# Scaling the fourth x tile of the opening on GpSimd in place of DVE

## The chip, the cores and the metric

The kernel runs on one core of one Trainium2 chip. The metric is the device time of one execution in microseconds (us); the median of several runs is given. The engines are named as the profile names them: PE (TensorE), ACT (ScalarE), DVE (VectorE), POOL (GpSimd) and SP, which here only issues DMAs.

## The reference

The kernel computes an attention block with a cached set of keys and values, gated by a SwiGLU block, with a residual:

```
xn = layernorm(x)                                  # x: 2048 x 640, bf16
q  = xn @ wq                                       # 32 heads of 192
p  = softmax(q @ k^T * 192**-0.5)                  # 2048 cached keys for each head
s  = concat_heads(p @ v) @ wo
g  = silu((silu(xn @ w1) * (xn @ w3)) @ w2)        # hidden width 1536
out = x + s * g
```

The layer norm is (x - mean) / sqrt(var + eps) for each row, without weights.

## The kernel before, in words

The 2048 rows of x are 16 tiles of 128 rows (`x_all[:, i, :]`). Each tile is normalised, turned so that its 640 columns stand on the partitions, and kept as `xnT[:, i]`; all projections read `xnT`. A query block (`qb`) is four tiles, 512 rows. The first four tiles are needed before any product can start, so the opening does them by themselves, and in another way than the other twelve:

- **Statistics.** Tiles 0, 2 and 3 get their mean and variance on DVE (`ln_stats`, `bn_stats` at L237 and `bn_aggr` at L240), tile 1 on ACT (L279 to L281). They land in `mv`.
- **Root.** `ln_root` (L246, L249) makes 1 / sqrt(var + eps) on ACT, for two tiles at a time: `ln_root(0)` for tiles 0 and 1, `ln_root(2)` for tiles 2 and 3.
- **Scaling.** `ln_scale(i)` (L257) computes (x - mean) * root in one `tensor_scalar` with two operations, a tile of 128x640 bf16 into a tile `xn` of the same shape. This is the step of the change.
- **Turning.** `ln_turn` makes five PE transposes for each tile (L264) into PSUM (`pst`); then ACT copies tiles 0 and 2 and DVE tiles 1 and 3 into `xnT` (L265).

Until the first tile is scaled, PE runs products of constants (`keep_busy`, L226). After the 20 transposes it goes on to the first products of head 0 (`pq`, `pf`, L318), first with tiles 0 and 1, then with tiles 2 and 3. The other tiles are scaled on DVE by the same function and turned by a DMA (`scale_and_turn`, L268).

The attention works on one head and one query block at a time, in eight steps (`p`) of 256 keys: scores on PE (`st`, L505) into one of two PSUM buffers, exponential on ACT (`pT`, L512), values on PE (`obank`, L545). The exponential subtracts a bound `nb` for the scores' maximum. For the first block of head 0, the bound comes from a small PE product (L438). For head 1, whose first block follows right behind, it comes from `next_bound(1, 0)`: two small DVE operations (L445, L448) and a sum over the partitions on GpSimd (`partition_all_reduce`, L451). This sum is one of GpSimd's loadable instructions; the kernel loads the library that has it at L73, as GpSimd's first instruction:

```
sums = next(x for x in all_libraries if bass_isa.InstPartitionAllReduce in x.instructions)
pin(nc.gpsimd.load_library(sums))
```

GpSimd has other work in the opening: it clears `st` (L163), puts ones into the values (L151), copies half of the keys to the other 64 partitions (`KS`, L154, in two halves for each of the first two heads) and rows of the queries (L379, L385).

`pin` keeps instructions in the order in which the code is written, for each engine. So the order of the opening is written out by hand, and an instruction of GpSimd's queue waits for all ahead of it. A load of a library for an instruction that needs another one than the last is put in by the language, right ahead of that instruction.

Of the kernel before, what the change touches and what calls it, by code (L numbers as in the profile page):

```python
# [30 lines left out]
def _kernel_impl(ctx, tc, A_x, A_k_cache, A_v_cache, A_wq, A_wo, B_w1, B_w3, B_w2, out):  # L31
    nc = tc.nc
# [33 lines left out]
    pin = tc.keep_in_program_order  # L66
# [108 lines left out]
    with ExitStack() as actx:  # L175
# [12 lines left out]
        mv = lnx.tile([P, NQT, nc.vector.BN_AGGR_DIM], F32, name="mv")  # L188
        x_all = lnx.tile([P, NQT, D], BF16, name="x_all")
# [52 lines left out]
        rstd = {}  # L242
# [9 lines left out]

        scaled = {}

        def ln_scale(i):
            scaled[i] = xnp.tile([P, D], BF16, tag="xn", name="xn")
            pin(nc.vector.tensor_scalar(out=scaled[i][:], in0=x_all[:, i, :], scalar1=mv[:, i, 0:1], scalar2=rstd[i],  # L257
                                        op0=ALU.subtract, op1=ALU.mult))

        def ln_turn(i, pool, tag, cp):  # L260
# [9 lines left out]
        def scale_and_turn(i):  # L270
            ln_scale(i)
            dma_turn(i)
# [16 lines left out]
        keep_busy(1, behind=ln_stats(3, lambda seen: keep_busy(1, behind=seen)))  # L289
        ln_root(2)  # L290
        for i in range(4):
            ln_scale(i)
        turned = []
        for i in range(4):
            pool, tag = (ps_st, "st2") if i < 2 else (ps_o, f"ob{3 - i}")
# [849 lines left out]
@with_exitstack  # L1145
def kernel(
    ctx: ExitStack,
    tc: tile.TileContext,
    A_x: bass.AP,
    A_k_cache: bass.AP,  # L1150
    A_v_cache: bass.AP,
    A_wq: bass.AP,
    A_wo: bass.AP,
    B_x: bass.AP,
    B_w1: bass.AP,
    B_w3: bass.AP,
    B_w2: bass.AP,
    out: bass.AP,
):
    _kernel_impl(ctx, tc, A_x, A_k_cache, A_v_cache, A_wq, A_wo, B_w1, B_w3, B_w2, out)  # L1160
# [30 lines left out]
```

## Time and profile before

| | us |
|---|---|
| median of 3 runs | 1932.29 (1932.17 to 1932.43) |
| profiled execution, own time | 1932.65 |
| its span, first to last instruction | 1931.1 |
| PE busy | 1924.4 |
| ACT busy | 1275.8 |
| DVE busy | 950.1 |
| GpSimd busy | 447.5 |

The granted TensorE clock was 1.0 over the span. Times in the views are counted from the start of the span. A row in order of time gives start, length, engine, line, operation, output and inputs, a count where like instructions are merged, and in brackets the idle time ahead of it and what ended it. A row of a group gives a count, busy time, mean ns of one, idle time and what ended it. A row of a source line gives the shortest, median and longest duration in ns and the first and last start. Rows marked with a q (POOLq) belong to the engine's sequencer and not to its busy time.

### The profile page before, as it was taken

What the parts mean: (1) busy time and instruction counts of PE and PEld (TensorE: products, weight loads), DVE (VectorE), ACT (ScalarE), POOL (GpSimd) and SP (SyncE); (2) the same over time, 40 slices, a digit from 0 to 9 for tenths busy, and PEclk for the clock granted to TensorE, in tenths of its full rate; (3) what the DMA queues carried; (4) which work ended last, traced back from release to release, by engine and by line L of the source; (5) the groups of instructions that cost most, each with busy time, mean ns of one, the idle gap of its engine ahead of it and who ended that gap; (6) DMA issues with size and microseconds to landing.
All of it is one profiled execution on the core that took longest, in us unless ns stands there. A gap on an engine that the chain in (4) does not pass through costs nothing.

```text
span 1931.1 us, 59187 instructions
## 1 busy us (share of the span) xinstructions
PE 1924.4 (100%) x26595; PEld 1266.7 (66%) x26621; DVE 950.1 (49%) x1794; ACT 1275.8 (66%) x1284; POOL 447.5 (23%) x756
## 2 busy tenths in 40 slices
PE   9999999999999999999999999999999999999999
PEld 6666666666666666666666666666777777444444
DVE  7765545554545554545555555555554544421111
ACT  7777777777777777777777777777777777210000
POOL 2432222222222222223222222222222210000000
PEclk9999999999999999999999999999999999999999
DMA  8422223131212222222422222213121102868752
GB/s 170 94 71 50 72 41 79 41 80 42 63 38 59 49 63 52 58 77 71 104 53 68 50 71 50 71 42 80 42 80 37 37 10 75 268 105 165 158 114 61
DMA packets 336835, 145.36 MB, mean 75 GB/s; under 512 B 286688, under 2 KB 330400, under 8 KB 336576
## 3 DMA queue, kind: packets, MB, share of 16 engines
q1 hardware_dynamic: 320592, 113.37, 25.8%
q0 software_dynamic: 7744, 23.60, 4.3%
q10 hardware_dynamic: 8240, 4.56, 0.8%
q8 instruction: 209, 3.42, 0.7%
q14 instruction: 50, 0.41, 0.1%
HBM read 56.23 MB, written 31.98 MB: 46 GB/s over the span
## 4 chain that ended last, share of the span: by engine, by line
PE 99%; DMA 0%; DVE 0%; issue 0%; SPq 0%
PE obank L545 35%; PE st L505 34%; PE ps L345 14%; PE ps_s L925 8%; PE ps_f L973 2%; PE ps_t L934 2%; PE ps_gu L318 1%; PE ps_s L948 1%; PE ps_gu L345 1%; PE ps_f L983 0%; DMA x_all<-in_A_x_dram 0%; DVE st L237 0%; PE pst L264 0%; PE pq L318 0%; PE pb L325 0%
## 5 line engine op out<-in xcount | busy, mean ns | idle before, releaser
L512 ACT ACTIVATE pT<-st,nb 128x1024 bf16<-128x1024 f32 x960 | 1068.5, 1113 | 327.6 <-PE st L505 323.8
L545 PEld LDWEIGHTS <-pT 64*128 64x128 bf16 x16384 | 717.5, 94 | 238.6 <-ACT pT L512 0.4
L545 PE MATMUL obank<-vt,pT 64*128 64x193 bf16 x16384 | 854.3, 243 | 0.0
L521 DVE TENSOR_REDUCE osum<-obank 128x386 f32<-128x772 f32 x256 | 234.2, 956 | 640.3 <-PE obank L545 640.3
L505 PE MATMUL st<-qF,KT 64*128 64x512 bf16 x1024 | 385.0, 376 | 0.0
L505 PE MATMUL st<-qD,KT 64*128 64x512 bf16 x1024 | 385.0, 376 | 0.0
L505 PE MATMUL st<-qS,KT 64*128 64x512 bf16 x1024 | 384.9, 376 | 0.0
L505 PE MATMUL st<-qS,KS 64*128 64x512 bf16 x1024 | 384.9, 376 | 0.0
L505 PE MATMUL st<-qA,KS 64*128 64x512 bf16 x1024 | 384.8, 376 | 0.0
L505 PE MATMUL st<-qA,KT 64*128 64x512 bf16 x1024 | 384.8, 376 | 0.0
L505 PEld LDWEIGHTS <-KT 64*128 64x128 bf16 x4096 | 288.5, 94 | 134.2
L345 PE MATMUL ps<-xnT,w 64*128 64x512 bf16 (+1 forms) x2540 | 313.5, 374 | 0.0
L379 POOL COPY qS<-qA 64x512 bf16<-64x512 bf16 x255 | 158.5, 622 | 564.6 <-ACT qA L389 555.1
L345 PEld LDWEIGHTS <-w 64*128 64x128 bf16 x2540 | 123.9, 94 | 116.9
L505 PEld LDWEIGHTS <-KS 64*128 64x128 bf16 x2048 | 177.0, 94 | 7.6
L925 PE MATMUL ps_s<-wo_sb,oT 128*128 128x512 bf16 x704 | 156.8, 379 | 0.8
L528 DVE TENSOR_TENSOR ostage<-osum,rl_all 128x384 bf16<-128x384 f32 x256 | 142.8, 558 | 8.9
L925 PEld LDWEIGHTS <-oT 128*128 128x128 bf16 x720 | 70.4, 98 | 84.5
L154 POOL COPY KS<-KT 64x1024 bf16<-64x1024 bf16 (+1 forms) x68 | 68.6, 1009 | 232.7 <-DMA KT<-in_A_k_cache_dram 200.6
L108 POOL DMA_DIRECT2D w<-in_A_wq_dram x60 | 52.9, 882 | 289.8 <-PE ps L345 289.6
L390 DVE CAST qF<-ps 128x512 bf16<-128x512 f32 x120 | 83.0, 691 | 72.3 <-ACT qA L389 72.3
L890 DVE SCALAR_TENSOR_TENSOR tmp<-ps_s,g_all 128x512 f32<-128x512 f32 x16 | 11.0, 688 | 177.4 <-PE ps_s L925 168.2
(112 smaller groups left out, 1148.6 us busy)
## 6 DMA issues: line engine op xcount, KB each, us to landing
o_scr<-ostage SPq DMA_DIRECT2D x64, 384.0 KB, 2.7
vt<-in_A_v_cache_dram SPq DMA_DIRECT2D x60, 384.0 KB, 5.0
wo_sb<-in_A_wo_dram POOLq DMA_DIRECT2D x1, 7680.0 KB, 31.1
w<-in_A_wq_dram POOLq DMA_DIRECT2D x30, 160.0 KB, 3.6
hT_scr<-hblk SPq DMA_DIRECT2D x16, 256.0 KB, 3.0
xt<-in_A_x_dram POOLq DMA_DIRECT2D x8, 320.0 KB, 4.4
w<-in_B_w_dram POOLq DMA_DIRECT2D x30, 80.0 KB, 2.6
w<-in_A_wq_dram POOLq DMA_DIRECT2D x30, 80.0 KB, 3.0
```

The lines of the kernel that those rows point to most:

```text
L108: return lambda eng: keep(eng.dma_start(out=w[:, :, c0:c1], in_=src[:, s0:s0 + c1 - c0].rearrange("(c p) d -> p c d", p=P)))
L154: return [keep(nc.gpsimd.tensor_copy(out=KS[ROWS[r], c0:c1], in_=ks[ROWS[1 - r], 2 * r, c0:c1])) for r in range(2)]
L345: mm = pin(nc.tensor.matmul(out[:, t * 512 + t0 * P:t * 512 + (t0 + step) * P], lhsT=ws[t][ROWS[r], c, :], rhs=rows_of(qb, c, ROWS[r], t0, ...
L379: return [lambda t=t: keep(copy(out=hd["qS"][ROWS[t], qs], in_=hd["qA"][ROWS[1 - t], qs])) for t in range(2)]
L390: pin(cast(out=hd["qF"][:, qs], in_=ps[:, 512:1024]))
L505: pin(nc.tensor.matmul(st2[:, t * 512:(t + 1) * 512], lhsT=k[ROWS[t]], rhs=q[ROWS[t], qs], start=(s == 0), stop=(s == 2)))
L512: pin(nc.scalar.activation(out=pT2[:, c0:c1], in_=st2[:, c0:c1], func=ACT.Exp, scale=SCALE, bias=nb))
L521: pin(nc.vector.tensor_reduce(out=osum[:], in_=ob[:].rearrange("p t (j c) -> p j c t", j=2)[:, :, 0:DH + 1, :], axis=AX.X, op=ALU.add))
L528: pin(nc.vector.tensor_tensor(out=ostage[:, b * 2:b * 2 + 2, hg * DH:(hg + 1) * DH], in0=osum[:, :, 0:DH], in1=rl.unsqueeze(2).to_broadcas ...
L545: pin(nc.tensor.matmul(acc["o"][b][:, r, j * 256:j * 256 + DH + 1], lhsT=pT2[ROWS[r], t * 512 + i * P:t * 512 + (i + 1) * P], rhs=vt[ROWS[ ...
L925: pin(nc.tensor.matmul(wide[t], lhsT=oT[:, j, t * P:(t + 1) * P], rhs=wo_sb[:, k, 0:WIDE], start=(k == 0), stop=(k == OC - 1)))
L934: pin(nc.tensor.matmul(turned, lhsT=wo_sb[:, k, WIDE:D], rhs=oT[:, j, 0:w], start=(k == 0), stop=(k == OC - 1)))
```

## The change

`ln_scale` gets a parameter for the engine, and the opening passes GpSimd for tile 3. Nothing else in the code changes.

```
-        def ln_scale(i):
+        def ln_scale(i, eng=nc.vector):
             scaled[i] = xnp.tile([P, D], BF16, tag="xn", name="xn")
-            pin(nc.vector.tensor_scalar(out=scaled[i][:], in0=x_all[:, i, :], scalar1=mv[:, i, 0:1], scalar2=rstd[i],
+            pin(eng.tensor_scalar(out=scaled[i][:], in0=x_all[:, i, :], scalar1=mv[:, i, 0:1], scalar2=rstd[i],
                                         op0=ALU.subtract, op1=ALU.mult))
...
         for i in range(4):
-            ln_scale(i)
+            ln_scale(i, nc.gpsimd if i == 3 else nc.vector)
```

On DVE, in the opening, `rstd_205` is the root of tiles 2 and 3 and `pst` the PSUM tile of the transposes (- is before, + is the change):

```order
 L240 BN_AGGR mv<-st_197 128x2
 L257 TENSOR_SCALAR xn<-x_all,mv,rstd_195 128x640 x2
-L257 TENSOR_SCALAR xn<-x_all,mv,rstd_205 128x640 x2
+L257 TENSOR_SCALAR xn<-x_all,mv,rstd_205 128x640
 L265 COPY xnT<-pst 128x640 x2
 L412 TENSOR_REDUCE st<-KT 128x1
```

One scaling is gone, and DVE comes to its two copies one instruction sooner.

On GpSimd, from its first instruction after the start of the kernel; `L73 ISA` is the load of the library with the partition sum, and `KS<-KT` is the copy of head 0's keys:

```order
 L73 ISA
 L163 MEMSET st 128x16 x2
+L257 ISA
+L257 TENSOR_SCALAR xn<-x_all,mv,rstd_205 128x640
 L151 MEMSET vt 128x16
 L154 COPY KS<-KT 64x512 x2
```

The scaling stands ahead of the memset and of the copies. With it comes an `ISA` row, which is an instruction of the same kind as the one at L73 and loads library 0, while L73 loads library 1.

On GpSimd, around its first partition sum (`nb_all<-ns` is the sum for the first block of head 1, the copies are those of the two halves of head 1's keys):

```order
 L151 MEMSET vt 128x16
 L154 COPY KS<-KT 64x512 x2
+L451 ISA
 L451 ISA nb_all<-ns 128x1
 L154 COPY KS<-KT 64x512 x2
```

The added `ISA` row loads library 1 again, ahead of the first sum and behind the copies of the first half of head 1's keys. The queues of PE, ACT and SP, SP's DMAs among them, are the same in both programs.

## The prediction

> **What bounds the kernel now.** I read the page first, then the chain of work that ended last, cut to the first 30 us, then the order of time around the fourth tile and around GpSimd's first partition sum. The page:
>
> ```profile
> span 1931.1 us, 59187 instructions
> PE 1924.4 (100%) x26595; PEld 1266.7 (66%) x26621; DVE 950.1 (49%) x1794; ACT 1275.8 (66%) x1284; POOL 447.5 (23%) x756
> PE 99%; DMA 0%; DVE 0%; issue 0%; SPq 0%
> ```
>
> TensorE (PE) is busy all the time and is 99% of the chain. So the sum is simple: whatever makes PE wait comes back almost whole in the time, and whatever frees DVE or GpSimd (POOL) at 49% and 23% is worth nothing unless PE was waiting for it. The profiled execution took 1932.65 us, 1.6 us of it outside the span; the median of the runs is 1932.29 us, 0.36 lower. I sum against 1932.65 and take 0.36 off at the end.
>
> The chain in the opening, in order of time (start, length, what):
>
> ```profile
> 7.28 0.39 PE fill L226
> 7.67 1.46 PE pst L264 x20
> 9.14 0.03 issue
> 9.17 0.71 PE pq L318 x5
> ```
>
> PE turns the four x tiles (L264, 20 transposes) and goes on to the first products without a gap. All 20 transposes stand ahead of the products, so the fourth tile's scaling has no cover: each 0.1 us by which it is late makes all that follows 0.1 us late. Around it:
>
> ```profile
> 7.14 1.49 DVE L257 TENSOR_SCALAR xn<-x_all,mv,rstd 128x640 bf16<-128x640 bf16 x4
> 7.59 0.20 ACT L249 ACTIVATE rstd<-lv 128x2 f32<-128x2 f32 x1
> 7.59 1.54 PE L264 MATMUL pst<-ident_bf,xn 128*128 128x128 bf16 x20
> 8.54 0.48 DVE L265 COPY xnT<-pst 128x640 bf16<-128x640 bf16 x1
> ```
>
> DVE scales the four tiles back to back and ends at 7.14 + 1.49 = 8.63. The root that the third and fourth need is there at 7.59 + 0.20 = 7.79.
>
> **The change part by part.** DVE loses one scaling, 1.49 / 4 = 0.37 us. That saves nothing by itself: DVE's copy at 8.54 could start sooner, but the products that read it stand behind the fourth tile's transposes.
>
> GpSimd gets the scaling. Its nearest rows are its copies:
>
> ```profile
> L154 POOL COPY KS<-KT 64x1024 bf16<-64x1024 bf16 x60 | 63.8, 1063 | 220.5 <-DMA KT<-in_A_k_cache_dram 196.9 <-PE ps L345 22.2
> L154 POOL COPY KS<-KT 64x512 bf16<-64x512 bf16 x8 | 4.9, 608 | 12.2 <-DVE xnT L265 8.3 <-DMA KT<-in_A_k_cache_dram 3.6
> ```
>
> 512 columns more cost 0.455 us, so a copy of 640 columns would be 0.608 + 128 x 0.89 ns = 0.72 us. That is the lower end; twice that per column, for two operations, gives 0.15 + 2 x 0.57 = 1.3 us as the upper end. I take 0.9, nearer to the rows that exist. With the root at 7.79 and nothing else in the way the tile would be ready between 8.55 and 9.15, so -0.1 to +0.5 us against 8.63, +0.1 with my value.
>
> The part that decides is something the diff doesn't show. The built program has two more rows on GpSimd that load a library: one ahead of the scaling, one ahead of the first partition sum (L451), which goes back to the library that L73 had loaded. What is known of a load:
>
> ```profile
> L73 POOLq MODIFY_POOL_CONFIG  x2: 11/11/11, 1.1 to 1.1; - x2
> 1.16 0.15 POOL L163 MEMSET st<- 128x16 f32 x2 [0.46 <-POOLq L1175]
> 1.24 0.16 POOL L151 MEMSET vt<- 128x16 bf16 x1
> ...
> 22.18 0.55 POOL L451 PARTITION_ALL_REDUCE nb_all<-ns  x1 [1.52 <-DVE ns L448]
> ...
> 36.53 0.39 POOL L451 PARTITION_ALL_REDUCE nb_all<-ns  x1 [0.37 <-DVE ns L448]
> ```
>
> The load at L73 is two rows of 11 ns at 1.1, and the memsets behind it run at once. Its first user, 21 us on, is 0.55 - 0.39 = 0.16 us longer than the next one. So a load that is real costs anything between about 0.2 us and the 21 us that lie between L73 and 22.18, or L73 loads nothing because the library is still there from the execution before. The second is likelier: no queue but the kernel's own moves anything in the first 16 us.
>
> ```profile
> DMA packets 8999, 3.54 MB, mean 221 GB/s; under 512 B 7975, under 2 KB 8999, under 8 KB 8999
> q1 hardware_dynamic: 8999, 3.54, 97.3%
> ```
>
> In the changed kernel the library really changes twice per execution. [...]
>
> ```profile
> KT<-in_A_k_cache_dram SPq DMA_TRANSPOSE x1, 6.3
> L108 POOL DMA_DIRECT2D w<-in_A_wq_dram x60 | 52.9, 882 | 289.8 <-PE ps L345 289.6 <-issue 0.2
> ```
>
> 6.3 + 0.9 = 7.2 us, an estimate, with 0.2 and 21 kept as the ends. [...]
>
> First load. It stands behind two memsets that end at 1.31 and waits for nothing, so it runs from 1.3 to 8.5, mostly under the statistics. The scaling then runs from 8.5 to 9.4 and the fourth tile is ready 0.8 us later than the 8.63 of before. PE goes on 0.8 us later.
>
> Second load. GpSimd's queue ahead of it, and what waits behind it:
>
> ```profile
> 17.62 0.17 POOL L151 MEMSET vt<- 128x16 bf16 x1
> 19.38 1.27 POOL L154 COPY KS<-KT 64x512 bf16<-64x512 bf16 x2 [1.59 <-DMA KT<-in_A_k_cache_dram]
> ...
> 22.79 1.26 POOL L154 COPY KS<-KT 64x512 bf16<-64x512 bf16 x2
> 24.15 1.11 ACT L512 ACTIVATE pT<-st,nb_all 128x1024 bf16<-128x1024 f32 x1 [0.27 <-PE st L505]
> 25.71 0.38 PE L505 MATMUL st<-qA,KT 64*128 64x512 bf16 x1
> ```
>
> The copies of head 1's keys wait for a transfer until 19.38, with 1.59 us of idle time that absorbs the 0.8, so they still end at 20.65. The load then runs from 20.65 to 27.85, the partition sum from 27.95 to 28.5, and only then can ScalarE (ACT) take the first exponential of head 1, which stood at 24.15. It ends at 28.55 + 1.11 = 29.66. PE, meanwhile, has its old values and the second scores to do, but the third scores need the score buffer that this exponential frees: they start at 29.7 in place of 25.71. That is **+4.0 us**, and it contains the first 0.8, since GpSimd's clock of events is set by the key transfer and not by PE. Generally the sum is the load's length less 3.2 us. The copies behind the sum (22.79, now 28.6 to 29.9) are wanted by the fifth scores of the block, at 28.74 before and 32.7 now: hidden, with 2.8 us to spare. PE has no idle time later in which to win the wait back. Later partition sums find their library in place.
>
> Sum: 1932.65 + 4.0 = 1936.65, or **1936.3** as a median.
>
> **The rivals.** *A switch is nearly free, so not slower.* If a load takes under 3.2 us the partition sum is still ready for 24.15 + 0.8, and if it takes under 6.5 the scaling doesn't wait for it. Then only GpSimd's own pace is left, -0.1 to +0.5, with up to 0.44 more if it must wait for DVE's third tile. A row bears on that:
>
> ```profile
> 11.62 0.29 DVE L379 COPY qS<-qA 64x512 bf16<-64x512 bf16 x1 [1.36 <-ACT qA L596]
> 11.65 0.73 POOL L379 COPY qS<-qA 64x512 bf16<-64x512 bf16 x1 [0.65 <-ACT qA L596]
> 15.74 0.61 POOL L379 COPY qS<-qA 64x512 bf16<-64x512 bf16 x1
> ```
>
> GpSimd's copy beside one of DVE took 0.12 us longer than the same copy alone. [...] Time: 1932.2 to 1933.2, 1932.5 likeliest. For it: 11 ns rows, and no transfer. Against: those rows can be loads that had nothing to do. A gain needs a scaling under 0.8 us; DVE's freed 0.37 us is the most it could be, far under 0.2%, which is about what a measurement of this kernel can tell from no change.
>
> *The load comes only when the first user is called.* Then nothing is hidden: the scaling is called at 7.85, loads until 15.05 and ends at 15.95, 7.3 us late. The partition sum is called when its input is there, 22.0 + 7.3 = 29.3; it loads until 36.5 and ends at 37.05; the exponential ends at 38.2, the third scores start then and not at 25.71 + 7.3 = 33.0, 5.2 more. Together +12.5: 1944.8. For it: the memsets behind L73 weren't held up. Against: the first sum's 0.55 us has no load in it. [...]
>
> *The load at L73 is real too, and the two stand in a row.* Then the second ends at 1.1 + 14.4 = 15.5, the scaling at 16.4, 7.8 us late. GpSimd's queue is behind PE's clock now: copies 25.6 to 26.9, third load until 34.1, exponential until 35.9 against 33.5: 2.4 more. Together +10.2: 1942.5. [...] For it: L73's load could run behind the memsets unseen. Against: no transfer in the queues.
>
> **How the numbers follow.** Forecast 0.42; a free switch 0.20; load at the call 0.18; two in a row 0.15; loads of over 10 us, 0.05. The range goes from the free switch without a gain, 1932.4, to 1944.5, which leaves out the top of the late load, the long loads and the gains, under 2 in 10. 0.2% is 3.9 us, so the line runs through the forecast, at a load of 7.1 us. Slower by over 0.2%: somewhat over half of the forecast (0.24) and all of the last three cases, 0.62. Within: the rest of the forecast and the free switch less the little that I keep for a gain, 0.36. Faster by over 0.2%: 0.02, for nothing that I can name.
>
> **What would show it.** In the changed profile I look for the start of GpSimd's scaling (8.5 by the forecast, 7.8 to 8.3 with a free switch, 15 by the others), the start of the first product (9.17 before, 10.0 by the forecast), GpSimd's first partition sum (22.18 before, 27.95), and ScalarE's idle time ahead of the exponential of 24.15 (0.27 before, some 3.6). The forecast is wrong if the scaling starts after 10 us, or if the exponential waits on PE as before, or if PE's wait at the third scores is given back later, against the 99%.

## The result and the profile after

The changed kernel took 1937.21 us (median of 11 executions, 1935.97 to 1944.30) against 1932.63 us before (11 executions): 1.0028 of the time before, 95% interval 1.0020 to 1.0036. It is slower, by 4.6 us between the medians; the ratio goes by all executions, whose means are 5.4 us apart. The forecast was 1936.3. The profiled execution took 1938.15 us with a span of 1936.5, 5.4 us more than the span before, and the readings below are of that one.

The page's first lines, after:

```profile
span 1936.5 us, 59218 instructions
PE 1928.0 (100%) x26621; PEld 1268.3 (65%) x26621; DVE 949.9 (49%) x1793; ACT 1276.7 (66%) x1284; POOL 451.4 (23%) x757
```

The totals hardly move. The instructions that differ take microseconds, and the time that is lost is idle time, so it has to be looked for in the first 35 us. GpSimd's rows there, after (start, length, engine, line, operation; in brackets the idle time ahead of the row):

```profile
1.16 0.15 POOL L163 MEMSET st<- 128x16 f32 x2 [0.46 <-POOLq L1175]
9.32 2.52 POOL L257 TENSOR_SCALAR xn<-x_all,mv,rstd 128x640 bf16<-128x640 bf16 x1 [8.00 <-ACT xnT L265]
11.80 0.16 POOL L151 MEMSET vt<- 128x16 bf16 x1
...
21.41 1.28 POOL L154 COPY KS<-KT 64x512 bf16<-64x512 bf16 x2
29.63 0.40 POOL L451 PARTITION_ALL_REDUCE nb_all<-ns  x1 [6.94 <-DMA xnT<-xn]
30.09 1.25 POOL L154 COPY KS<-KT 64x512 bf16<-64x512 bf16 x2
```

The two library loads have rows in the engine's sequencer, of 3 to 7 ns, which tell where a load begins and nothing of its length:

```profile
L257 POOLq MODIFY_POOL_CONFIG  x2: 3/5/7, 1.3 to 1.3; - x2
L451 POOLq MODIFY_POOL_CONFIG  x2: 4/4/4, 22.9 to 22.9; - x2
```

The loads themselves are the 8.00 us of idle time ahead of the scaling and the 6.94 us ahead of the first partition sum. The releasers named there (an ACT copy, a DMA) have nothing to do with either instruction: they are what happened to end last before it. The sum had its input `ns` at 26.66, and the scaling its root at 7.29:

```profile
7.09 0.20 ACT L249 ACTIVATE rstd<-lv 128x2 f32<-128x2 f32 x1
```

PE in the opening and at the first block of head 1, after:

```profile
7.10 1.19 PE L264 MATMUL pst<-ident_bf,xn 128*128 128x128 bf16 x15
11.89 0.45 PE L264 MATMUL pst<-ident_bf,xn 128*128 128x128 bf16 x5 [3.60 <-POOL xn L257]
12.18 0.71 PE L318 MATMUL pq<-xnT,w 128*128 128x256 bf16 x5
...
31.23 0.37 PE L505 MATMUL st<-qA,KT 64*128 64x512 bf16 x1 [0.67 <-ACT pT L512]
```

PE waits 3.60 us for the fourth tile. Its first product comes at 12.18, 3.0 us later than the 9.17 of before, although the opening ran half a microsecond sooner in this execution (the root of tiles 2 and 3 at 7.29 against 7.79). The third scores of head 1's first block come at 31.23, 5.5 us later than the 25.71 of before, and the span is 5.4 us longer: all of the loss has happened by then.

Between these two points something else happens. The products of L318 by shape, first before, then after (count, busy time, mean ns of one):

```profile
L318 PE MATMUL pf<-xnT,w 128*128 128x256 bf16 x10 | 1.4, 273 | 0.0
L318 PE MATMUL pa<-xnT,w 128*128 128x512 bf16 x5 | 1.2, 379 | 0.0
```

```profile
L318 PE MATMUL pf<-xnT,w 128*128 128x256 bf16 x10 | 2.2, 373 | 0.0
L318 PE MATMUL pa<-xnT,w 128*128 128x512 bf16 x5 | 1.7, 489 | 0.0
```

The same products are slower by about a third. The granted clock in windows, after (window, length, PE busy, clock, DMA share, GB/s):

```profile
12.50:12.80 0.30, 0.30 (x5) 1.00 1.46 81
13.10:16.30 3.20, 3.20 (x16) 0.50 1.11 244
16.60:17.00 0.40, 0.40 (x4) 1.00 1.08 320
```

PE is back at work at 11.89; 1.2 us later the clock is halved, from 13.1 to 16.5, for 3.4 us, which costs half of that, 1.7 us. Here it fell after a wait of 3.60 us; in the last run below it fell after one of 1.87 us. The spread of the 11 executions goes with it: the fastest, 1935.97, has a mean granted clock of 1.000, the nine others up to 1938.28 have 0.999, and the slowest, 1944.30, has 0.997.

So two things make PE late before it comes to the wait for the sum. Its last values ahead of that wait, first before, then after, and the exponential behind the sum:

```profile
23.88 1.34 PE L545 MATMUL obank<-vt,pT 64*128 64x193 bf16 x28
```

```profile
28.57 1.34 PE L545 MATMUL obank<-vt,pT 64*128 64x193 bf16 x28
30.06 3.20 ACT L512 ACTIVATE pT<-st,nb_all 128x1024 bf16<-128x1024 f32 x3 [1.49 <-POOL nb_all L451]
```

PE is 4.7 us late there: 3.0 from the fourth tile and 1.7 from the clock. The wait for the sum adds 0.8 us, and from then on the lateness stays: the last exponential of the kernel starts at 1646.55, 5.5 us later than the 1641.09 of before.

### The profile page after: what moved, and what is told of

Its sections match the earlier page's. It is cut to its first block, busy times and chain, and to the rows that moved or that the text cites. A ratio compares the mean times of both kernels' runs of the same rounds, so it can differ in the third digit from the quotient of the medians.

```text
span 1936.5 us, 59218 instructions
## 1 busy us (share of the span) xinstructions
PE 1928.0 (100%) x26621; PEld 1268.3 (65%) x26621; DVE 949.9 (49%) x1793; ACT 1276.7 (66%) x1284; POOL 451.4 (23%) x757
## 4 chain that ended last, share of the span: by engine, by line
PE 99%; ACT 0%; DMA 0%; DVE 0%; issue 0%; POOL 0%; ACTq 0%
PE obank L545 35%; PE st L505 34%; PE ps L345 14%; PE ps_s L925 8%; PE ps_f L973 2%; PE ps_t L934 2%; PE ps_gu L318 1%; PE ps_s L948 1%; PE ps_gu L345 1%; PE ps_f L983 1%; ACT pT L512 0%; DMA xnT<-xn 0%; PE pf L318 0%; PE pq L318 0%; PE pa L318 0%
```

## The experiments

The theory at the outset: the time is made of a late fourth tile (load and slow scaling), a stretch of half clock behind PE's wait, and the second load, which delays the partition sum; the last two of these run side by side with what follows the first, so that the later one counts. The rivals are that GpSimd's instruction alone is slow and loads are cheap, that a load is paid at the first call, and that the delays add up. The runs compare with the kernel before on the same chip, 1932.6 to 1932.8 us. Of each run the median and the ratio with its 95% interval are given.

**The loads alone.** DVE scales all four tiles; the load stands where the change has it, and the language puts the second one ahead of the partition sum.

```
+        pin(nc.gpsimd.load_library(standard))
         for i in range(4):
             ln_scale(i)
```

> DVE scales all four tiles as before; only the two library loads of the change are there. Theory A (both loads cost time, the first one hides under the statistics): the opening is as before, first product near 9.2 us; GpSimd's first partition sum starts some 6.8 us after its load is issued at 20.8, near 27.6, and the third scores of that block come 3.5 us late: 1936.1 us. Rival B (a load costs little, GpSimd's scaling is what is slow): within 0.3 us of the kernel before, 1932.6 us.

1938.56 us, 1.0035 (1.0021 to 1.0048): the loads alone cost as much as the change, if not more (1.0028; the intervals overlap). GpSimd:

```profile
9.24 0.16 POOL L152 MEMSET vt<- 128x16 bf16 x1 [7.93 <-DMA KT<-in_A_k_cache_dram]
...
28.39 0.40 POOL L453 PARTITION_ALL_REDUCE nb_all<-ns  x1 [7.57 <-DVE st L238]
```

The opening is as before (first product at 9.19). The memset is the telling row. It waits for nothing and runs with either library (at 11.80 in the changed kernel, behind the load of library 0), it ran at 1.24 behind the load at L73 in the kernel before, and here it stands 7.93 us behind the load. So the load that changed the library held up GpSimd's queue from where it stood, also for an instruction that runs with either library. The time is above the 1936.1 expected for two reasons: the second load was 0.8 us longer than assumed, and PE waited 4.1 us for the exponential and then lost half of the following 3.4 us to the clock (the first row gives the wait in total, how often, and the longest):

```profile
PE st L507 <- ACT pT L514: 4.1, 1, 4.1
```

```profile
31.50:34.00 2.50, 2.50 (x25) 0.50 0.82 255
```

**The scaling without a load.** GpSimd copies the tile; the normalisation of these 128 rows is left out.

```
+            if i < 3:
+                ln_scale(i)
+        scaled[3] = xnp.tile([P, D], BF16, tag="xn", name="xn")
+        pin(nc.gpsimd.tensor_copy(out=scaled[3][:], in_=x_all[:, 3, :]))
```

> GpSimd copies the fourth tile with tensor_copy in place of scaling it, so no library is loaded (the normalisation of this tile is left out). Theory A: the copy starts near 7.9 us (its input is there sooner, but it stands where the scaling stood), lasts 0.72 us, and the time is within 0.5 us of the kernel before, 1932.6 us. Rival B (any 128x640 instruction on GpSimd is slow in this stretch, beside DVE's scalings): it lasts 2 us or more and the time is 1934 us or more.

1932.58 us, 1.0000 (0.9991 to 1.0009). The copy needs no statistics, so it ran at 5.94 and lasted 0.72 us. This bounds what the change could have gained: with the fourth tile ready at 6.66 in place of 8.63, and DVE freed of the scaling, the kernel is not measurably faster. The first product came 0.28 us sooner, at 8.89; PE lost that again at 32.08, where it waited 0.44 us for a tile turned by a DMA.

**An early call.** A 128x1 `tensor_scalar` on constants ahead of the scaling.

```
+        early_call = lnx.tile([P, 1], F32, name="early_call")
+        pin(nc.gpsimd.tensor_scalar(out=early_call[:], in0=eps_t[:], scalar1=eps_t[:], scalar2=eps_t[:], op0=ALU.subtract,
+                                    op1=ALU.mult))
```

> A 128x1 tensor_scalar on constants stands on GpSimd right behind the first load, ahead of the scaling of the fourth tile. Theory A1 (part of the load is paid by the first call, after its input is there): the small instruction takes that part, the scaling starts as soon as its input is there, near 7.9 us, and PE's wait falls from 3.6 to under 2.2 us; the second load then costs more of its own, and the time is near 1936.0 us. Theory A2 (the load runs from its issue on, whoever calls): the scaling starts at 9.3 us as in the changed kernel, 1937.2 us.

1938.80 us, 1.0029 (1.0018 to 1.0039).

```profile
8.96 0.40 POOL L284 TENSOR_SCALAR early_call<-eps_t 128x1 f32<-128x1 f32 x1 [7.65 <-DVE xnT L265]
9.36 2.53 POOL L257 TENSOR_SCALAR xn<-x_all,mv,rstd 128x640 bf16<-128x640 bf16 x1
```

The small call has its operands from 1.3 us on and still runs only at 8.96, and the scaling behind it starts as late as in the changed kernel and lasts as long. Theory A2: no part of the load waits for the call's input, and 2.5 us hold no first-call cost. The time is above the 1937.2 expected: four executions with a mean clock of 0.999 took 1936.94 to 1937.84 us, the profiled one among them, and five with 0.998 took 1938.80 to 1939.63. Why the clock was lower in these isn't shown.

**PE kept busy.** 16 products of constants ahead of the fourth tile's transposes.

```
+            if i == 3:
+                warm = ps_o.tile([P, 2, 512], F32, tag="ob0", name="warm")
+                for _ in range(16):
+                    pin(nc.tensor.matmul(warm[:, 0, :], lhsT=one_l, rhs=one_r[:, 0:512], start=True, stop=True))
             turned.append(ln_turn(
```

> The changed kernel with 16 products of constants on PE ahead of the fourth tile's transposes, 3.4 us in which PE was idle. Theory A (the products behind the wait are slow because the granted clock falls to 0.5 after the idle stretch, some 1.7 us in most executions): the granted clock stays at 1.0, the first products last 0.27 us each as before, and the time is near 1935.9 us with a spread under 1 us. Rival B (they are slow for another reason, weights or rows that come late): 1937.2 us or more.

1936.81 us, 1.0021 (1.0012 to 1.0030). All 11 executions have a granted clock of 1.000 and lie within 1.2 us, so the half clock came from the idle stretch. But the time fell by 0.4 and not by 1.3 or more. The chain shows where the rest went (start, length, what). Between 27.5 and 29.1 it names what happened to end; what the sum waited for is the load, which stands behind key copies that end at 21.41:

```profile
12.26 0.55 PE pq L322 x5
...
26.97 0.52 PE obank L549 x12
27.52 0.97 DVE osum L525
28.49 0.65 issue
29.14 0.41 POOL nb_all L455
29.58 1.12 ACT pT L516
30.74 0.82 PE st L509 x6
```

```profile
29.14 0.40 POOL L455 PARTITION_ALL_REDUCE nb_all<-ns  x1 [7.73 <-DVE osum L525]
```

PE, now faster, arrives sooner at the partition sum and waits there. Its third scores start at 30.74, half a microsecond before those of the changed kernel. GpSimd came to the second load 1.3 us sooner too (21.41 against 22.69), but the load lasted 7.73 us in place of 6.94. So most of what the clock gave back was lost to the second load.

**No wait for the second load.** The first block of head 1 subtracts head 0's bound, in the changed kernel; loads and sum stay.

```
+            if (h, qb) == (1, 0):
+                hd["nb"][0] = heads[0]["nb"][0]
```

> The changed kernel, with the first block of head 1 subtracting head 0's bound (which is there already) in place of its own, so that its exponentials don't wait for the partition sum behind the second load; the sum itself and both loads stay. Theory A (the two delays lie side by side on one clock: the opening's lateness and the second load, and the later one counts): the wait for the sum goes, but the opening's lateness and the slow clock behind it stay, 3.0 + 1.7 us in most executions: 1936.4 to 1937.3 us, 0 to 0.8 us less than the changed kernel. Rival B (the two add up, the second load is worth some 3 us by itself): 1934.5 us or less.

1937.75 us, 1.0027 (1.0017 to 1.0036), no gain against the changed kernel's 1.0028. PE has no wait at the exponential any more, and its third scores stand at 30.23 in place of 31.23. So the late tile and the half clock by themselves bring PE to within 1 us of where the second load would have stopped it. Of that 1 us the span of the profiled execution kept 0.4 (1936.1). The rest went later: the first exponential of the next block, at 33.15 before, starts 4.52 us late here (37.67), the last one of the kernel 5.05 us late (1646.14 against 1641.09). In all four runs with this edit the lateness grows by these 0.5 us, and in none of the others. So they belong to the edit; how it costs them isn't shown.

**Both.** PE kept busy, and head 0's bound.

> Both edits together: PE kept busy through the wait for the fourth tile (16 products of constants), and head 0's bound for the first block of head 1. Theory A: only the lateness of the fourth tile is left, first product near 12.26 against 9.17 less the 0.5 us by which the opening came sooner there: 1935.3 to 1935.8 us. Rival B (other work that waits for GpSimd, such as the key copies behind the second load, is late too): 1936.5 us or more.

1936.86 us, 1.0020 (1.0011 to 1.0029), over the 1935.3 to 1935.8 expected. That is where the rival put the time, but not for its reason: the granted clock of the profiled execution is 1.0 and PE waits for nothing of GpSimd's later. The opening itself was later than in the run with PE kept busy alone:

```profile
9.41 2.52 POOL L257 TENSOR_SCALAR xn<-x_all,mv,rstd 128x640 bf16<-128x640 bf16 x1 [8.10 <-DVE xnT L265]
```

```profile
9.03 3.66 PE L299 MATMUL warm<-const-bfloat16-1.0 128*128 128x512 bf16 x16
12.74 0.44 PE L264 MATMUL pst<-ident_bf,xn 128*128 128x128 bf16 x5
13.02 0.71 PE L322 MATMUL pq<-xnT,w 128*128 128x256 bf16 x5
```

The load took 8.10 us, and the 16 products, started later, ended 0.8 us behind the scaling's 11.93. The first product at 13.02 is 3.85 us later than before, and the run is 4.1 us slower (the profiled span is 4.4 us longer): here the opening is nearly the whole loss, 0.8 us of it through the added products, and the rest is the 0.5 us of the bound's edit.

**Both loads, and nobody who waits for the sum.** DVE scales, both loads stand, head 0's bound.

> DVE scales all four tiles, both loads are there, and the first block of head 1 subtracts head 0's bound. Theory A (a load costs only through who waits for GpSimd, and here nobody does): within 0.4 us of the kernel before, 1932.6 us, with both loads at 7 to 8 us in the trace. Rival B (a load also slows others, by its transfer or by holding the key copies behind it): 1934 us or more.

1935.34 us, 1.0014 (1.0005 to 1.0023): the rival's side. With the sum out of the way, the next to wait is PE, for the key copies queued behind it:

```profile
30.10 1.25 POOL L155 COPY KS<-KT 64x512 bf16<-64x512 bf16 x2
```

```profile
31.41 0.39 PE L509 MATMUL st<-qA,KS 64*128 64x512 bf16 x1 [1.95 <-POOL KS L155]
```

These copies ended at 31.35 and had been wanted at 29.1. The load, 7.83 us here, has two users behind it, and taking one away shows the other. The profiled execution, 1937.53, is the slowest of the 11 and has a mean clock of 0.999; the eight with 1.000 took 1934.35 to 1936.03.

**The same library again.** The kernel before, with one more load of the resident library ahead of the sum.

```
+            if (h, qb) == (1, 0):
+                pin(nc.gpsimd.load_library(sums))
```

> The kernel before with one more load of the library that is there already, ahead of the first partition sum. Theory A (a load of the resident library does nothing): two rows of some 10 ns, the sum at its old place near 22.2 us, and 1932.6 us. Rival B (each load instruction fetches): the sum near 28 us and 1937 us or more.

1932.69 us, 0.9999 (0.9990 to 1.0008). The added load moves nothing: the span is 1931.1 as before, and the sum, at 22.72 (22.18 before), stands 0.96 us behind key copies that a transfer had released later, as it does in the run with the copied tile, which has no added load. The load of what was there was free, so L73 in the kernel before, with a memset right behind it at 1.24, loaded nothing, and its 11 ns said nothing about the price of a change.

**GpSimd's pace.** A look at five instructions behind the scaling, on the same tile.

```
+        pin(nc.gpsimd.tensor_scalar(out=probe[:], in0=x_all[:, 3, :], scalar1=mv[:, 3, 0:1], scalar2=rstd[3],
+                                    op0=ALU.subtract, op1=ALU.mult))
...
+        pin(nc.gpsimd.tensor_copy(out=probe[:], in_=x_all[:, 3, :]))
```

> A look at durations on GpSimd. Behind the scaling of the fourth tile stand, on the same tile: the scaling again, one subtraction with a scalar per partition, one subtraction with a constant, the scaling of 320 columns, and a copy of 640. The time of the whole is of no use. Theory A (the 2.52 us are GpSimd's pace for this instruction, per column): the repeat lasts 2.5 us, 320 columns 1.3 to 1.4, the copy 0.72. Rival B (they hold a first-call cost or a wait for DVE): the repeat lasts under 1.5 us.

```profile
11.41 2.49 POOL L294 TENSOR_SCALAR probe<-x_all,mv,rstd 128x640 bf16<-128x640 bf16 x1
14.00 1.88 POOL L296 TENSOR_SCALAR probe<-x_all,mv 128x640 bf16<-128x640 bf16 x1
15.97 1.81 POOL L297 TENSOR_SCALAR probe<-x_all 128x640 bf16<-128x640 bf16 x1
17.89 1.43 POOL L298 TENSOR_SCALAR probe<-x_all,mv,rstd 128x320 bf16<-128x320 bf16 x1
19.39 0.72 POOL L300 COPY probe<-x_all 128x640 bf16<-128x640 bf16 x1
```

2.5 us is the steady price: (2.49 - 1.43) / 320 = 3.3 ns for each column, and 0.37 us fixed. A single operation on the tile is 1.8 to 1.9 us whether its scalar is a tensor or a constant. A copy has 0.89 ns for each column, by the rows of the kernel before.

**The first load taken out of the opening.** The kernel loads library 0 in an idle stretch late in the execution, at 1592 us, so that the next execution finds it; only the load ahead of the sum is left in the opening.

```
-    pin(nc.gpsimd.load_library(sums))
+    pin(nc.gpsimd.load_library(standard))
...
+                    if (h, qb, p) == (H - 1, 1, 4):
+                        pin(nc.gpsimd.load_library(standard))
```

> The changed kernel, but it loads the scaling's library (0) at its start and again near its end, in an idle stretch of GpSimd behind the last partition sum, so that the library is already there when the next execution begins; only the load ahead of the first partition sum is left in the opening. Theory A: the scaling starts when its root is there, near 7.9 us, and ends near 10.4; the fourth tile is 1.7 us late, too little for the clock to fall; the load ahead of the partition sum starts near 20.8 and the sum near 28.3, so the third scores of that block come some 4.2 us late: 1936.5 to 1937 us, not better than the changed kernel, since the second load now sets the end. Rival B (the two loads add up): 1934 us or less.

1937.51 us, 1.0026 (1.0017 to 1.0035). The scaling starts at 7.92 and PE's wait for the fourth tile is halved (1.87 us), and nothing is won:

```profile
7.92 2.69 POOL L257 TENSOR_SCALAR xn<-x_all,mv,rstd 128x640 bf16<-128x640 bf16 x1 [6.44 <-DVE xn L257]
...
29.46 0.40 POOL L451 PARTITION_ALL_REDUCE nb_all<-ns  x1 [7.66 <-DVE st L237]
```

```profile
ACT pT L512 <- POOL nb_all L451: 4.2, 1, 4.2
PE st L505 <- ACT pT L512: 3.4, 1, 3.4
```

The second load now sets the end by itself, as in the first experiment. The clock of the profiled execution stayed at 1.0 behind both waits of PE (1.87 and 3.4 us). That 1.7 us is too little for a fall was the author's estimate: no run shows a length below which the clock stays, and the next run's fell after 1.87 us.

**The slow scaling alone.** The same, with head 0's bound.

> The same, and the first block of head 1 subtracts head 0's bound, so that nobody waits for the partition sum. Theory A: what is left is GpSimd's pace in the scaling, 1.7 us, and perhaps some tenths where the fifth scores of the block wait for the key copies behind the load: 1934.3 to 1935.3 us, granted clock 1.0. Rival B (GpSimd's scaling itself costs nothing, all is the loads): 1932.7 us.

1936.27 us, 1.0012 (1.0003 to 1.0021). The executions fall into two groups by clock: four at 1.000 with 1934.90 to 1935.26, as expected, and seven at 0.999 with 1936.22 to 1936.81, which was not. PE's wait for the fourth tile in the profiled execution:

```profile
10.57 0.45 PE L264 MATMUL pst<-ident_bf,xn 128*128 128x128 bf16 x5 [1.87 <-POOL xn L257]
```

Without a fall of the clock the run is 2.1 to 2.5 us slower (against 1932.76). Of this, 1.7 us are GpSimd's pace, by the first product at 10.86 in place of 9.17, and 0.5 us come with the edit of the bound, as above. Where the clock falls, it is some 1.4 us more.

## Why the prediction was right, and where its sum was off

The direction and the cause held: two loads that the diff doesn't show are by themselves enough for the loss. The forecast was 4.0 us, the medians give 4.6 and the profiled execution 5.5. That the sum came so near is in part luck: it was made of 0.8 us for the late tile and 3.2 for the second load, and in the profiled execution it was 4.7 for the late tile and the clock, and 0.8 for the second load. By its own steps:

- **The load is real and about 7.2 us: right.** In ten profiled executions with the change's loads it was 6.35 to 8.10 us of idle time on GpSimd, the first one 7.53 to 8.10 (in eight), the second 6.35 to 7.83 (in nine). The 7.2 were the author's estimate, a transfer of 6.3 us and an issue of 0.9, and came out well; that a load is made of these no run shows: during the first one, from 1.1 to 9.4 us, only the kernel's own queue moved data (1.70 MB, 1.69 before).
- **L73 loads nothing: right,** shown by the free second load and by the memset that a real load holds up. With that the rival of two loads in a row falls. The rival of a load at the first call falls with the changed kernel's own row, the scaling at 9.32 and not at 15, and with the memset that waits behind the load; the free switch falls with the loads alone. The load ran from where it stands, before the call had its input: in the changed kernel the second begins at 22.69, the sum has its input at 26.66 and starts at 29.63.
- **The first load hides under the statistics: mostly.** It ended at 9.3 in place of 8.5, and the root was there at 7.3.
- **The scaling takes 0.9 us: the term that was mis-sized.** It takes 2.52. The step that failed is the upper end, "twice that per column, for two operations": a copy's row was taken for the pace of all GpSimd work, and `tensor_scalar` costs 3.3 ns for each column, nearly four times a copy's. So the fourth tile came at 11.84 and not at 9.4, and the first product 3.0 us late in place of 0.8.
- **The clock: not foreseen.** The forecast let PE wait and go on at full speed. In six profiled executions a wait of 1.87 to 4.10 us was followed by 3.4 us at half clock; in two others waits of 1.87, 1.9 and 3.4 us were not.
- **The second load starts at 20.65: wrong, for the same reason.** The 1.59 us of slack ahead of the key copies would have absorbed 0.8 us, not 3.0 and the slow clock. The copies ended at 22.69, the sum started at 29.63 in place of 27.95, and the third scores at 31.23 in place of 29.7. The idle time of ScalarE ahead of the exponential was 1.49 us, where 3.6 had been expected.
- **The delays don't add: right.** With the wait for the sum taken away (1.0027), or the first load (1.0026), or the half clock (1.0021), the time stays about where it was, because another delay is right behind. It falls by half only where two are gone that leave little behind: the scaling and the wait for the sum (1.0014), the first load and the wait for the sum (1.0012). Both of these hold the 0.5 us of the bound's edit.
- **PE can't win the wait back: right.** PE was 5.5 us late at the third scores, and the last exponential is as late.
- **DVE's freed time is worth nothing: right,** as far as a measurement can tell: the copied tile has 1.0000, 0.9991 to 1.0009.

## What to carry to other kernels

Before an instruction is moved to GpSimd, look in the built program for a library load that comes with it, and for the one that brings the old library back; here each held up the queue of that engine for 6.35 to 8.10 us, and the price was set by who waited behind it. Take an engine's pace from the same operation, not from a copy of the same shape (2.52 us here against 0.72). Where PE waits for microseconds, count a stretch of half clock behind it too (here 3.4 us of it, a loss of 1.7, behind waits of 1.87 to 4.10 us in six profiled executions; in two there was none), and where several delays run side by side, expect that removing one shows the next (1.0021 to 1.0027 here, with one gone, against 1.0028).

## What the runs showed of the hardware that was not expected

- A load of the resident library was free (1932.69 us against 1932.78); the 11 ns of its rows at L73 don't show that, since those of a real load took 3 to 7 ns. And a library stayed from one execution to the next: with library 0 loaded near the end, the next execution's scaling started at 7.92 in place of 9.32.
- GpSimd's `tensor_scalar` of 128x640 bf16 with two operations lasted 2.49 to 2.69 us, 5.7 to 6.1 times DVE's 0.44 for a tile of the same shape.
- The clock fell to 0.50 after a wait of PE of only 1.87 us in the profiled execution of the last run, and stayed at 1.00 after the same wait in that of the run before it. So the length of the wait doesn't decide it alone.
